# Zero products ahead of the first input, and two more PSUM banks for the first stage, in a spectral-filter and MLP kernel

## The chip, the cores and the metric

The kernel runs on one core of a Trainium2 chip. The metric is the device time of one execution in microseconds (us), the median of several executions. Times inside a profile count from the start of its span.

## The reference

```python
# x: (8, 3008, 256); filt_r, filt_i: (1505, 256); w_in: (256, 2048); w_out: (2048, 256); alpha: (2048)
X = np.fft.rfft(x, axis=1)
y = np.fft.irfft(X * (filt_r + 1j * filt_i), n=3008, axis=1).reshape(24064, 256)
h = y @ w_in
s = np.sin(alpha * h)
out = (h + s * s / (alpha + 1e-09)) @ w_out
```

The kernel does the Fourier transform as matrix products in three stages, batch by batch. Stage 1 (products `pa`) goes through a DRAM buffer (`d1`, stored from `t1`, reloaded as `t2`), stage 2 (products `pb` and `pc`, filter between them) goes through another (`d2`, reloaded as `t4`), and stage 3 (`pd`) gives `y`. Then come the hidden layer (`ph`, a sine, a square) and the projection (`po`). While the MLP of one batch runs, the three stages of the next are woven in between, following a plan in steps. Only the first batch's stages stand alone: they are the prologue.

## The kernel before

```python
fps = pool("fps", 2, PSUM); hps = pool("hps", 2, PSUM); ops = pool("ops", 2, PSUM)
...
def load_x(b):                       # four input chunks, cast to fp16 by the DMA, GpSimd queue
    for ch in range(4):
        ins = nc.gpsimd.dma_start(out=xt, in_=...)
        if b == 1:
            after(ins, marks["t4"])
...
def stage1(u):
    ch, half = divmod(u, 2)
    ...
    for i in range(2):
        n0 = 4 * half + 2 * i
        ps = fps.tile([128, 512], FP32, name=f"pa_{b}_{u}_{i}", tag="f")
        marks["pe"] = nc.tensor.matmul(out=ps[0:NK, :], lhsT=wf_t, rhs=st["x"][ch][:, n0:n0 + 2, :],
                                       start=True, stop=True)
        evac(st["t1"][:, n0:n0 + 2, :], ps[0:NK, :])      # ScalarE and VectorE in turn
    if half == 1:
        nc.sync.dma_start(out=d1_rows[:, 8 * ch:8 * ch + 8, :], in_=st["t1"])
    if u == 7:
        ...   # reload: t2[g], g = 0..3, one half each on the SyncE and (batch 0) the ScalarE queue
...
first = spectral(0)
for _, piece in first[:8]:           # stage 1 of batch 0
    piece()
after(nc.sync.dma_start(out=d_t, in_=d_dram.ap()), marks["x", 1])    # 768 KB table for stage 2
...
for g in range(4):                   # filter rows, GpSimd queue
    for k, filt in enumerate((filt_r, filt_i)):
        for q in range(2):
            ins = nc.gpsimd.dma_start(out=f_t[k][32 * q:32 * q + 32, 6 * g:6 * g + 6, :], in_=...)
            if g >= 2:
                after(ins, marks["t2", g - 2])
...
w_out32 = vpool.tile([128, 16, C], FP32, name="w_out32", tag="v")
after(nc.gpsimd.dma_start(out=w_out32, in_=...), marks["t4"])        # output weights, 2 MB
...
plan = {1: [-45 + i for i in range(8)],
        2: [-29 + 14 * i / 13 for i in range(13)],
        3: [-10, -9] + [-7 + 2 * i for i in range(14)]}
...
        at_step = 48 * b + plan[stage][at[stage]]
        if b == 1 and stage == 1:
            at_step = 9 + at[stage]
```

Of the kernel before, what the change touches and what calls it, by code (L numbers as in the profile page):

```python
# [9 lines left out]
FP16 = mybir.dt.float16  # L10
FP32 = mybir.dt.float32
# [43 lines left out]
def kernel(  # L55
# [10 lines left out]
    nc = tc.nc  # L66
# [17 lines left out]
    def pool(name, bufs, space=None):  # L84
        kw = {} if space is None else {"space": space}
        return ctx.enter_context(tc.tile_pool(name=name, bufs=bufs, **kw))

    cpool = pool("consts", 1)
# [10 lines left out]
    fps = pool("fps", 2, PSUM)  # L99
    hps = pool("hps", 2, PSUM)  # L100
    ops = pool("ops", 2, PSUM)
# [11 lines left out]
    def load_x(b):  # L113
        tiles = []
        for ch in range(4):
            xt = xpool.tile([NR, 8, C], FP16, name=f"x_{b}_{ch}", tag="x")
            ins = nc.gpsimd.dma_start(
                out=xt,
                in_=bass.AP(tensor=x.tensor, offset=x.offset + (b * S + ch * 8) * C,
                            ap=[[32 * C, NR], [C, 8], [1, C]]),  # L120
            )
            if b == 1:
                after(ins, marks["t4"])
            if b == 0:
                marks["x", ch] = ins
            tiles.append(xt)
        return tiles
# [3 lines left out]
    def evac(dst, src, on_act=None):  # L131
        flip[0] ^= 1
        if flip[0] if on_act is None else on_act:
            marks["act"] = nc.scalar.copy(out=dst, in_=src)
        else:
            marks["dve"] = nc.vector.tensor_copy(out=dst, in_=src)

    def spectral(b):
# [8 lines left out]
        def stage1(u):  # L147
            ch, half = divmod(u, 2)
            if u == 0:
                st["x"] = load_x(b)  # L150
            if half == 0:
                st["t1"] = t1pool.tile([NK, 8, C], FP16, name=f"t1_{b}_{ch}", tag="t1")
            for i in range(2):
                n0 = 4 * half + 2 * i
                ps = fps.tile([128, 512], FP32, name=f"pa_{b}_{u}_{i}", tag="f")
                marks["pe"] = nc.tensor.matmul(out=ps[0:NK, :], lhsT=wf_t, rhs=st["x"][ch][:, n0:n0 + 2, :],  # L156
                                               start=True, stop=True)
                evac(st["t1"][:, n0:n0 + 2, :], ps[0:NK, :])
# [3 lines that stand above are left out]
                st["t2"] = []  # L162
                for g in range(4):
                    t2 = t2pool.tile([128, 6, C], FP16, name=f"t2_{b}_{g}", tag="t2")
                    for p in range(2):
                        a0 = p * NS + 6 * g
                        eng = nc.scalar if b == 0 and p else nc.sync
                        marks["t2", g] = eng.dma_start(out=t2[64 * p:64 * p + 64, :, :],
                                          in_=d1[a0:a0 + 6, :, :].rearrange("s n c -> n s c"))
                    st["t2"].append(t2)  # L170
# [53 lines left out]
        for u in range(8):  # L224
            pieces.append((1, lambda u=u: stage1(u)))
# [11 lines left out]
    warm = cpool.tile([128, 1], FP32)  # L237
    nc.vector.memset(warm, 0.0)
    nc.scalar.activation(out=warm, in_=warm, func=AFT.Sin)

    first = spectral(0)
    for _, piece in first[:8]:
# [12 lines left out]
    for i in range(2):  # L255
        al_row.append(opool.tile([128, 2, C], FP32, name=f"al_row_{i}", tag="o"))
        for h in range(2):
            nc.scalar.dma_start(
                out=al_row[i][64 * h:64 * h + 1].rearrange("p a b -> p (a b)"),
# [10 lines left out]
    for g in range(4):  # L270
        for k, filt in enumerate((filt_r, filt_i)):
            for q in range(2):
                off, step = ((6 * g) * C, C) if q == 0 else ((N1 - 6 * g) * C, -C)
                ins = nc.gpsimd.dma_start(  # L274
                    out=f_t[k][32 * q:32 * q + 32, 6 * g:6 * g + 6, :],
# [20 lines left out]
    ps = fps.tile([128, 512], FP32, name="ps_rec", tag="f")  # L296
# [3 lines left out]
    for i in range(2):  # L300
        al_bc.append(hps.tile([128, 2, 512], FP32, name=f"al_bc_{i}", tag="h"))
        for h in range(2):
            behind(nc.tensor.matmul(out=al_bc[i][:, h, :], lhsT=ones[64 * h:64 * h + 1, :],
                                    rhs=al_row[i][64 * h:64 * h + 1].rearrange("p a b -> p (a b)"),
                                    start=True, stop=True), s1_pe)
# [17 lines left out]
    for i in range(2):  # L323
        for cb in range(2):
            behind(nc.vector.tensor_tensor(
                out=w1[:, cb, 1024 * i:1024 * i + 1024], in0=w_in32[:, cb, 1024 * i:1024 * i + 1024],
# [152 lines left out]
```

## Time and profile before

| | before |
|---|---|
| time, median of 3 (range) | 883.07 us (882.7 to 884.4) |
| span of the profiled run | 881.2 us |
| last store of stage 1: issued | 17.30 us |
| reload of it: issued | 22.49 us |
| first stage-2 product | 26.86 us |
| output weights first used | 64.38 us |
| first projection product | 74.19 us |
| first stage-2 product of batch 1, TensorE's wait before it | 104.19 us, 3.15 us |

The busy times by stretch follow. The columns after the length are busy us and number of instructions for TensorE, its weight loads, VectorE, ScalarE and GpSimd, then the granted TensorE clock, the DMA share (1.00 is all 16 engines busy) and GB/s.

```profile
core 0: us, PE busy (x) PEld busy (x) DVE busy (x) ACT busy (x) POOL busy (x), PEclk, DMA share, GB/s
...
11.00:16.00 5.00, 3.67 (x9) 1.27 (x8) 2.75 (x4) 2.13 (x4) 0.57 (x1) 1.00 1.05 274
16.00:22.00 6.00, 6.00 (x30) 3.55 (x31) 4.30 (x9) 2.91 (x4) 0.00 (x0) 1.00 1.05 286
22.00:24.00 2.00, 2.00 (x6) 0.66 (x2) 1.05 (x3) 0.25 (x1) 0.00 (x0) 1.00 0.01 4
...
200.00:800.00 600.00, 599.71 (x4553) 424.73 (x4551) 357.31 (x625) 375.97 (x482) 178.33 (x346) 1.00 0.42 102
```

From 200 to 800 us TensorE rests 0.29 us in all, so there is little to shorten but the prologue. In the prologue the DMA engines are full until 22 us and then empty for two: the reload may be issued only when the last store has landed (issued at 22.49 us), and its first bytes move 1.3 us later, near 23.8 us.

The chain of waits that ended last, in order of time (start, length, what):

```profile
14.57 0.60 PE pa_6_1_163 L156
15.16 0.02 issue
15.19 0.70 DVE t_0_3_159 L136
15.89 0.04 issue
15.93 0.60 PE pa_7_1_169 L156
16.53 0.02 issue
16.55 0.70 DVE t_0_3_159 L136
...
17.30 5.03 DMA d_0_107<-t_0_3_159
...
23.21 4.29 DMA t_0_1_176<-d_0_107
...
52.01 12.34 DMA w_out_502<-in_moe_w_out_dram
```

Product and eviction alternate one by one, which is what two banks allow when VectorE owns one of them. The store after them takes 5.03 us for 384 KB.

### The profile page before, as it was taken

How to read it: one execution, taken by the hardware profiler on the slowest of the kernel's cores; microseconds unless marked ns; L12 is line 12 of the kernel's file. 1: busy time of each engine (PE TensorE's matmuls, PEld its weight loads, DVE VectorE, ACT ScalarE, POOL GpSimd, SP SyncE). 2: the span in 40 equal slices, each digit the busy share in tenths (PEclk: the TensorE clock that was granted, in tenths of full speed). 3: DMA queues.
4: the chain of work that ended last, by engine and by line, in shares of the span. 5: the costliest groups of instructions: out<-in, count | busy, mean ns of one | idle time of the engine just before them, and what ended most of it. 6: DMA issues, size and time to landing. Idle time of an engine off the chain costs nothing.

```text
span 881.2 us, 15647 instructions
## 1 busy us (share of the span) xinstructions
PE 839.1 (95%) x6233; PEld 585.2 (66%) x6233; DVE 503.9 (57%) x886; ACT 521.1 (59%) x671; POOL 255.3 (29%) x495
## 2 busy tenths in 40 slices
PE   6759899999999999999999999999999999999993
PEld 2336677667776677767776677767776677667673
DVE  4737575566646565465756566565755666455441
ACT  4545565566656665666656666566656666555550
POOL 3211223333233232332233323233232232333332
PEclk9969999999999999999999999999999999999997
DMA  9984834185334724175343823256242533311111
GB/s 217 246 236 87 194 79 108 51 171 119 84 110 114 156 69 117 54 152 123 79 123 91 179 71 99 75 131 150 68 115 67 134 77 79 108 37 33 36 42 32
DMA packets 82737, 94.99 MB, mean 108 GB/s; under 512 B 12700, under 2 KB 64932, under 8 KB 82664
## 3 DMA queue, kind: packets, MB, share of 16 engines
q1 hardware_dynamic: 57008, 50.36, 22.0%
q0 software_dynamic: 23728, 42.77, 21.7%
q10 hardware_dynamic: 1928, 0.86, 0.5%
q8 instruction: 49, 0.80, 0.4%
q14 instruction: 24, 0.20, 0.1%
HBM read 58.02 MB, written 49.81 MB: 122 GB/s over the span
## 4 chain that ended last, share of the span: by engine, by line
PE 89%; DMA 6%; DVE 2%; issue 1%; ACT 0%; POOL 0%; SPq 0%; POOLq 0%; DVEq 0%
DMA w_out_502<-in_moe_w_out_dram 1%; DMA t_1_0_939<-d_1_504 1%; DMA d_7_517<-g_9_8756 1%; DMA d_0_107<-t_0_3_159 1%; DMA x_0_109<-in_x_dram 1%; DMA t_7_0_8931<-d_7_517 1%; DMA t_0_1_176<-d_0_107 0%; DMA t_0_0_476<-d_0_108 0%; PE po_0_5494 L390 0%; PE po_0_7950 L390 0%; PE po_2_4348 L390 0%; PE po_2_838 L390 0%; PE po_2_1892 L390 0%; PE po_0_705 L390 0%; PE po_0_4463 L390 0%
## 5 line engine op out<-in xcount | busy, mean ns | idle before, releaser
L375 PEld LDWEIGHTS <-w_465 128*128 128x128 f16 x1536 | 150.3, 98 | 100.4 <-issue 2.3
L198 PEld LDWEIGHTS <-e_t 128*128 128x128 f16 x384 | 37.5, 99 | 12.8 <-issue 2.5
L394 PEld LDWEIGHTS <-y 128*128 128x128 f16 x376 | 36.7, 98 | 4.7
L179 PEld LDWEIGHTS <-d_t 128*128 128x128 f16 x192 | 18.7, 100 | 27.6 <-DMA t_0_0_173<-d_0_107 3.5
L156 PEld LDWEIGHTS <-wf_t 94*96 94x96 f16 x128 | 16.5, 129 | 18.8 <-issue 9.4
L380 DVE TENSOR_TENSOR v_9644<-v_9644 128x1024 f16<-128x1024 f16 x8 | 5.5, 693 | 8.0 <-ACT v_9644 L379 8.0
L380 DVE TENSOR_TENSOR v_9789<-v_9789 128x1024 f16<-128x1024 f16 x8 | 5.5, 693 | 8.0 <-ACT v_9789 L379 8.0
L380 DVE TENSOR_TENSOR v_9488<-v_9488 128x1024 f16<-128x1024 f16 x8 | 5.5, 693 | 7.7 <-ACT v_9488 L379 7.7
L380 DVE TENSOR_TENSOR v_3898<-v_3898 128x1024 f16<-128x1024 f16 x8 | 5.5, 691 | 7.1 <-ACT v_3898 L379 7.1
L380 DVE TENSOR_TENSOR v_8810<-v_8810 128x1024 f16<-128x1024 f16 x8 | 5.5, 690 | 7.1 <-ACT v_8810 L379 7.1
L380 DVE TENSOR_TENSOR v_2681<-v_2681 128x1024 f16<-128x1024 f16 x8 | 5.5, 690 | 7.1 <-ACT v_2681 L379 7.1
L380 DVE TENSOR_TENSOR v_7593<-v_7593 128x1024 f16<-128x1024 f16 x8 | 5.5, 690 | 7.1 <-ACT v_7593 L379 7.1
L380 DVE TENSOR_TENSOR v_6354<-v_6354 128x1024 f16<-128x1024 f16 x8 | 5.5, 690 | 7.1 <-ACT v_6354 L379 7.1
L380 DVE TENSOR_TENSOR v_1442<-v_1442 128x1024 f16<-128x1024 f16 x8 | 5.5, 690 | 7.1 <-ACT v_1442 L379 7.1
L380 DVE TENSOR_TENSOR v_5137<-v_5137 128x1024 f16<-128x1024 f16 x8 | 5.5, 690 | 7.1 <-ACT v_5137 L379 7.1
L380 DVE TENSOR_TENSOR v_1608<-v_1608 128x1024 f16<-128x1024 f16 x8 | 5.5, 693 | 7.1 <-ACT v_1608 L379 7.1
L380 DVE TENSOR_TENSOR v_6520<-v_6520 128x1024 f16<-128x1024 f16 x8 | 5.5, 693 | 7.1 <-ACT v_6520 L379 7.1
L380 DVE TENSOR_TENSOR v_8976<-v_8976 128x1024 f16<-128x1024 f16 x8 | 5.5, 692 | 7.1 <-ACT v_8976 L379 7.1
L380 DVE TENSOR_TENSOR v_9147<-v_9147 128x1024 f16<-128x1024 f16 x8 | 5.5, 692 | 7.1 <-ACT v_9147 L379 7.1
L380 DVE TENSOR_TENSOR v_9317<-v_9317 128x1024 f16<-128x1024 f16 x8 | 5.5, 692 | 7.1 <-ACT v_9317 L379 7.1
L380 DVE TENSOR_TENSOR v_4064<-v_4064 128x1024 f16<-128x1024 f16 x8 | 5.5, 692 | 7.1 <-ACT v_4064 L379 7.1
L274 POOL DMA_DIRECT2D filt_101<-in_filt_r_dram x8 | 4.6, 587 | 16.9 <-DMA t_0_0_173<-d_0_107 15.0
(2527 smaller groups left out, 2688.4 us busy)
## 6 DMA issues: line engine op xcount, KB each, us to landing
w_in_469<-in_moe_w_in_dram POOLq DMA_DIRECT2D x2, 1024.0 KB, 9.2
w_out_502<-in_moe_w_out_dram POOLq DMA_DIRECT2D x1, 2048.0 KB, 12.3
filt_101<-in_filt_r_dram POOLq DMA_DIRECT2D x8, 96.0 KB, 7.0
filt_102<-in_filt_i_dram POOLq DMA_DIRECT2D x8, 96.0 KB, 7.4
d_t<-d_tbl SPq DMA_DIRECT2D x1, 768.0 KB, 7.9
d_0_107<-t_0_0_117 SPq DMA_DIRECT2D x1, 384.0 KB
d_0_107<-t_0_1_131 SPq DMA_DIRECT2D x1, 384.0 KB, 6.5
d_0_107<-t_0_2_145 SPq DMA_DIRECT2D x1, 384.0 KB
```

The source lines that it names most:

```text
L156: marks["pe"] = nc.tensor.matmul(out=ps[0:NK, :], lhsT=wf_t, rhs=st["x"][ch][:, n0:n0 + 2, :], start=True, stop=True)
L179: nc.tensor.matmul(out=ps[:, i, :], lhsT=d_t[:, s, :], rhs=st["t2"][s // 6][:, s % 6, :], start=True, stop=True)
L198: nc.tensor.matmul(out=ps[:, i, :], lhsT=e_t[:, k, 2 * w + i, :], rhs=pr[k][:, i, :], start=(k == 0), stop=(k == 1))
L274: ins = nc.gpsimd.dma_start(out=f_t[k][32 * q:32 * q + 32, 6 * g:6 * g + 6, :], in_=bass.AP(tensor=filt.tensor, offset=filt.offset + off, ...
L375: marks["hidden"] = nc.tensor.matmul(out=ps[:, i, 0:n], lhsT=w1[:, cb, jb * 128:jb * 128 + 128], rhs=y_cols[:, cb, c0:c0 + n], start=(cb = ...
L380: marks["square"] = nc.vector.tensor_tensor(out=vs, in0=vs, in1=vs, op=ALU.mult)
L394: nc.tensor.matmul(out=dst, lhsT=y_cols[:, cb, c0 + 128 * t:c0 + 128 * t + 128], rhs=m_t[:, cb, :], start=False, stop=(cb == 1))
```

## The change

Its intent: feed TensorE with products of zeros from 1.2 us on, so that its clock is up when the first input lands near 6 us; and let stage 1 of the first batch run on four banks, two for each evicting engine, so that product and eviction overlap.

```diff
-                ps = fps.tile([128, 512], FP32, name=f"pa_{b}_{u}_{i}", tag="f")
+                ps = (ops if b == 0 and i else fps).tile(
+                    [128, 512], FP32, name=f"pa_{b}_{u}_{i}", tag="o" if b == 0 and i else "f")
@@
+    zeros = cpool.tile([128, 512], FP16)
+    nc.vector.memset(zeros, 0.0)
+    idle = hps.tile([128, 2, 512], FP32, name="idle", tag="h")
+    for i in range(12):
+        nc.tensor.matmul(out=idle[:, 0, :], lhsT=zeros[:, 0:128], rhs=zeros, start=True, stop=True)
+
     first = spectral(0)
```

## The prediction

> **What bounds the kernel now.** Busy times by stretch: TensorE works 599.71 of the 600 us from 200 to 800, at clock 1.00. The change touches none of that, only the prologue (first 70 us), where the chain of waits runs through DMAs: first input load 1.25 to 5.92 us; stage 1 until 17.25, its last steps repeating product 0.60, VectorE eviction 0.69, on two PSUM banks; last store of stage 1 17.30 to 22.33; reload until 27.5; stage 2, bound by VectorE (4.9 of each 5 us); store, reload, 12.34 us load of the output weights; TensorE from 69 us.
>
> **What the change does.**
> - Twelve 128x512 products of zeros. Such products take 0.58 us in stage 1 and 0.38 later, so the clock is halved at first although the clock row prints 1.00. In stage 1 unhindered products start 0.38 to 0.43 apart, so twelve take about 5.1 us from about 1.3, ending near 6.4; if the clock rises meanwhile, near 5.6. The Trainium skill ("TensorE: Matmul & The Clock Gate", "What's actually happening") says about 3.4 us of sustained work lifts it; here full speed comes at 31.2 us, after 2.6 us of dense products. The input lands at 5.9: at worst stage 1 starts 0.5 us late, absorbed.
> - Four banks: two for ScalarE (0.58 us), two for VectorE (0.69). Four products (one input chunk) need about 1.4 us instead of 2.7. But chunks land 1.9 us apart (5.9, 7.7, 9.5, 11.4), so stage 1 becomes bound by input. Its last store is issued near 13.5 to 14.0 instead of 17.30.
>
> **How much is on the critical path.** Hardly any, because that store does not wait only for its issue. The DMA share is 1.0 or more from 4 to 21 us. The SyncE queue holds, in order, the 768 KB table (issued 7.74, landed 15.9) and the four 384 KB stores (issued 9.14, 11.85, 14.58, 17.30). It moves nothing until 11 us, while the input loads fill the engines, then 0.14 to 0.29 MB every microsecond until 21.8, 2.37 MB in all: exactly table and stores. The second store landed at 18.35, so the queue was never empty when the last came. The Trainium skill ("DMA: Bandwidth & Descriptors", "Queues, rings and completion order") says an engine consumes a ring in order and takes turns between queues by packet[...]. Earlier issues lengthen the backlog; the last landing moves only as far as stores get ahead of the filter loads on GpSimd's queue (0.25 MB between 19 and 21 us, at 0.3 MB per us at most 0.8 us: an estimate). I expect 0.5 us, and perhaps 0.3 from warmer products at 28 to 31 us, where VectorE is nearly full anyway. What is gained there passes down the chain.
>
> **Prediction.** 883.07 - 0.9 = 882.2 us; 8 in 10 between 879.8 and 883.6. Faster by over 2%: 0.005; within 2%: 0.99; slower: 0.005.
>
> **What would show it.** Stage 1's last eviction ends near 13.5 to 14 instead of 17.25 (banks). The last store, issued early, lands at 21.5 to 22.3, its wait grown from 5.0 to about 8 us (backlog). First stage-2 product at 26.3 to 26.9 (before: 26.86). TensorE from 100 us on unchanged.
>
> **What would make it wrong.** If the stores overtake filter loads or table, or deeper queues move more bytes per microsecond, the gain could reach 2 to 3.5 us. If earlier stores delay the table (needed at 16.3) or filter rows, or the zeros outlast the input, it could be 0.5 us slower.

## The result, and the profile after

The changed kernel took 881.20 us (880.19 to 882.96, 4 runs) against 883.74 us (882.7 to 885.41, 4 runs). The ratio is 0.9972, with a 95% interval of 0.9948 to 0.9995. A ratio is the mean time of one kernel's fast runs over the mean of the other's in the same rounds, so it is not quite the ratio of the medians. The same stretches after the change:

```profile
core 0: us, PE busy (x) PEld busy (x) DVE busy (x) ACT busy (x) POOL busy (x), PEclk, DMA share, GB/s
...
11.00:16.00 5.00, 4.18 (x9) 1.25 (x9) 3.38 (x5) 1.66 (x4) 0.57 (x1) 0.59 1.07 276
16.00:22.00 6.00, 6.00 (x31) 3.40 (x31) 2.94 (x7) 2.96 (x3) 0.00 (x0) 0.50 1.06 290
22.00:24.00 2.00, 0.87 (x3) 0.00 (x0) 0.87 (x3) 0.00 (x0) 0.00 (x0) 0.50 0.28 81
...
200.00:800.00 600.00, 600.00 (x4556) 425.38 (x4555) 357.27 (x625) 376.37 (x482) 177.33 (x344) 1.00 0.42 101
```

The DMA engines work at the same rate up to 22 us (276 and 290 GB/s against 274 and 286). The clock column cannot be compared here: in the profile of the kernel before the clock records begin at 31.2 us, and a stretch without a record is printed as 1.00, although its products take 0.58 us; with the zeros the records begin at 5.1 us. The chain:

```profile
2.95 8.96 DMA x_3_130<-in_x_dram
...
11.95 0.66 PE pa_6_0_175 L158
12.62 0.43 PE pa_7_0_181 L158
13.04 0.43 PE pa_6_1_178 L158
13.47 0.43 PE pa_7_1_184 L158
13.90 2.00 PE al_bc_274 L313 x2
...
20.80 0.97 ACT e_t L296
...
21.89 4.25 DMA t_0_0_188<-d_0_122
...
51.66 12.65 DMA w_out_517<-in_moe_w_out_dram
```

Stage 1 now waits for its last input, as forecast. The chain no longer names the store, but that is a coincidence: a ScalarE eviction of stage-2 tables happens to end at the time of the store's landing, 21.8 us. What released both halves of the reload is the landing. SyncE's half is issued at 21.87 and ScalarE's at 21.89 us, and in twelve of the fourteen profiles ScalarE's half follows SyncE's by 0.02 us, whenever that eviction ends (in zeros only it ends 0.1 us after the issue). The store and the first use of its data, VectorE's first use of the output weights, and TensorE's wait in batch 1, before and after:

```profile
17.30 0.30 SPq L160 DMA_DIRECT2D d_0_107<-t_0_3_159  x1
...
26.86 0.61 PE L179 MATMUL pb_0_267<-t_0_0_173,d_t 128*128 128x256 f16 x2 [1.97 <-DMA t_0_0_173<-d_0_107]
...
64.38 1.14 DVE L338 TENSOR_SCALAR w_466<-w_out_502,rec_t 128x256 f16<-128x256 f32 x4 [2.30 <-DMA w_out_502<-in_moe_w_out_dram]
...
104.19 0.38 PE L179 MATMUL pb_0_1020<-t_1_0_939,d_t 128*128 128x256 f16 x2 [3.15 <-DMA t_1_0_939<-d_1_504]
```

```profile
14.86 0.30 SPq L162 DMA_DIRECT2D d_0_122<-t_0_3_174  x1
...
26.19 0.61 PE L181 MATMUL pb_0_282<-t_0_0_188,d_t 128*128 128x256 f16 x2 [3.32 <-DMA t_0_0_188<-d_0_122]
...
64.33 1.14 DVE L348 TENSOR_SCALAR w_481<-w_out_517,rec_t 128x256 f16<-128x256 f32 x4 [2.85 <-DMA w_out_517<-in_moe_w_out_dram]
...
102.66 0.38 PE L181 MATMUL pb_0_1035<-t_1_0_954,d_t 128*128 128x256 f16 x2 [1.67 <-DMA t_1_0_954<-d_1_519]
```

The number in brackets is the idle time of the engine before the instruction. The last store is issued 2.44 us earlier, and stage 2 starts only 0.67 us earlier. At the output weights 0.05 us of that is left, and then 1.5 us appear at batch 1's reload, and 0.5 us near 754 us at that of a later batch, which the change does not touch. So this one pair of profiles puts most of its 2.0 us difference in a place that has nothing to do with the change, and the experiments had to tell whether that was its doing.

### The profile page after: what moved, and what is told of

It reads as the page before. It is cut to its first block, busy times and chain, and to the rows that moved or that the text cites. A ratio compares the mean times of both kernels' runs of the same rounds, so it can differ in the third digit from the quotient of the medians.

```text
span 879.2 us, 15673 instructions
## 1 busy us (share of the span) xinstructions
PE 840.8 (96%) x6245; PEld 586.7 (67%) x6245; DVE 503.8 (57%) x887; ACT 520.6 (59%) x671; POOL 255.1 (29%) x495
## 3 DMA queue, kind: packets, MB, share of 16 engines
q0 software_dynamic: 23728, 42.77, 21.8%
## 4 chain that ended last, share of the span: by engine, by line
PE 91%; DMA 5%; DVE 1%; ACT 1%; issue 1%; POOL 1%; SPq 0%; POOLq 0%; DVEq 0%; ACTq 0%
DMA w_out_517<-in_moe_w_out_dram 1%; DMA x_3_130<-in_x_dram 1%; DMA t_0_0_491<-d_0_123 0%; DMA t_1_0_954<-d_1_519 0%; DMA t_0_0_188<-d_0_122 0%; PE al_bc_274 L313 0%; PE po_0_7965 L400 0%; PE po_0_5509 L400 0%; PE po_2_6819 L400 0%; PE po_2_1907 L400 0%; PE po_0_720 L400 0%; PE po_2_4363 L400 0%; PE po_0_3053 L400 0%; PE po_0_2022 L400 0%; PE po_0_9170 L400 0%
```

## The experiments

Twelve kernels ran, all with correct results, in three groups of four; a group shared a chip and 11 runs of the kernel before. Theory A: the DMA backlog lets only 0.6 us or so through, the rest of the difference is scatter of later waits. Theory B: the change gains 2 us or more each time, by way of batch 1's reload. Each kernel has one profile. These are its waypoints in us; "before" and "changed" are the two kernels above:

| kernel | first `pa` | reload issued | first `pb` | weights used | first `po` | wait in batch 1 |
|---|---|---|---|---|---|---|
| before | 5.96 | 22.49 | 26.86 | 64.38 | 74.19 | 3.15 |
| before, again | 5.96 | 22.49 | 26.63 | 64.78 | 74.59 | 2.82 |
| before, shift | 6.11 | 22.47 | 26.78 | 64.77 | 74.58 | none |
| before, shift, input held | 6.10 | 22.54 | 26.95 | 64.40 | 77.43 | 0.48 |
| changed | 6.42 | 21.87 | 26.19 | 64.33 | 74.14 | 1.67 |
| changed, again | 6.32 | 21.39 | 25.50 | 62.81 | 72.62 | 3.14 |
| changed, shift | 6.18 | 21.73 | 26.10 | 64.56 | 74.36 | 0.40 |
| changed, shift, input held | 6.33 | 22.03 | 26.26 | 63.62 | 76.78 | 1.15 |
| zeros only | 6.45 | 22.64 | 27.30 | 63.84 | 73.65 | 1.94 |
| zeros only, shift | 6.43 | 22.65 | 27.02 | 65.38 | 75.18 | 1.01 |
| banks only | 6.12 | 22.33 | 26.47 | 64.42 | 74.23 | 2.31 |
| banks only in order, shift | 5.96 | 21.54 | 25.65 | 64.79 | 74.60 | 0.18 |
| before, shift, filter held | 6.09 | 20.52 | 28.21 | 65.73 | 75.54 | none |
| changed, shift, filter held | 6.30 | 20.73 | 25.75 | 64.16 | 73.97 | none |

### Changed kernel again

No edit.

> The changed kernel once more. Theory A (the prologue's gain is about 0.6 us at the first stage-2 product, and is lost again in the wait for the output weights; the 2 us that the two profiles differ by come from batch 1's reload, 4.37 us against 5.85, whose length varies from run to run): the first stage-2 product near 26.2 us, the first psm product within 0.4 us of the kernel before, the TensorE wait before pb_0 of batch 1 anywhere from 1.5 to 3.3 us, and a ratio between 0.996 and 1.001. Theory B (the gain of 2 to 2.5 us belongs to the change and is the same each time): TensorE wait before batch 1's pb_0 again 1.5 to 1.9 us and a ratio of 0.9965 to 0.998.

Measured: 882.35 us (881.13 to 882.81) against 883.80 us, ratio 0.9974 (0.9942 to 1.0005). The first stage-2 product came at 25.50 us, 0.7 earlier than theory A had it, and the first `po` 1.6 us before that of the first profile of before, so here the prologue's gain did pass the output weights. The wait in batch 1 was 3.14 us: theory B's repeat of 1.5 to 1.9 us did not come (nor does the interval, which reaches 1, show a gain by itself).

### Kernel before again

No edit.

> The kernel before, unchanged, as a control: ratio 1.000 within 0.002 under both theories. Theory A: its profile's TensorE wait before batch 1's first stage-2 product is not again 3.15 us but anywhere from 1.5 to 3.3. Theory B: again 2.9 to 3.3 us. Output weights used from 69 us under both.

Measured: 883.74 us (880.16 to 884.97) against 883.80 us, ratio 0.9985 (0.9954 to 1.0017). By the medians the two are alike; the ratio is below one because one of the 11 runs of the other took 891.08 us. The wait in batch 1 was 2.82 us, just outside theory B's range. With it, and in the changed kernel's repeat, came something new. The instruction that ended the wait in this profile, and the busy times of the stretches after it:

```profile
104.25 0.58 PE L179 MATMUL pb<-t,d_t 128*128 128x256 f16 x2 [2.82 <-DMA t<-d]
```

```profile
104.00:105.00 1.00, 0.75 (x7) 0.65 (x8) 0.00 (x0) 0.07 (x1) 0.56 (x2) 0.50 1.26 221
105.00:106.00 1.00, 1.00 (x7) 0.68 (x6) 0.81 (x2) 0.51 (x1) 0.00 (x0) 0.50 1.26 249
106.00:107.00 1.00, 1.00 (x6) 0.59 (x4) 1.00 (x3) 0.00 (x0) 0.00 (x0) 0.50 1.06 274
```

The two products take 0.58 us here and 0.38 us in the first profile of before: the clock (0.50) had fallen during the wait. It can be priced. From the first `po` to the start of the last two `po` products TensorE does the same work in every kernel, so that time, less the waits, should be nearly constant. It is 866.89 - 74.19 - 3.15 - 0.29 = 789.26 us in the first profile of before and 864.85 - 74.14 - 1.67 = 789.04 us in the changed kernel. It is 867.87 - 74.59 - 2.82 = 790.46 us here and 866.25 - 72.62 - 3.14 = 790.49 us in the changed kernel's repeat. These two are also the only ones of all fourteen profiles in which the clock fell there; in the ten not named here the same sum gives 789.05 to 789.77 us. A wait of 2.8 to 3.2 us in batch 1 was therefore followed by a further loss of 0.7 to 1.4 us in two of three cases, and by none in one.

### Zeros only

```diff
-                ps = (ops if b == 0 and i else fps).tile(
-                    [128, 512], FP32, name=f"pa_{b}_{u}_{i}", tag="o" if b == 0 and i else "f")
+                ps = fps.tile([128, 512], FP32, name=f"pa_{b}_{u}_{i}", tag="f")
```

> Only the twelve products of zeros, two banks as before. Both theories: the products of stage 1 take 0.38 us while the clock stays up, but two banks still make each pair wait for VectorE (about 1.1 us a pair instead of 1.36, if the clock stays up; 1.36 if it falls), so the last store is issued at 15 to 17 us and the SyncE queue drains at 21.3 to 21.8 as before. First stage-2 product at 26.3 to 26.9. Time: theory A 0 to 1 us under the kernel before, the same as with banks alone; theory B, if the zeros are what gains, 2 us under.

Measured: 883.14 us (880.83 to 884.71), ratio 0.9982 (0.9951 to 1.0012). First stage-2 product at 27.30 us, later than expected and than in any profile of the kernel before (26.63 to 26.95 us). The zeros ran until 6.3 us and the input landed near 6.4 us; the clock was at 0.71 between 9 and 10 us and at 0.50 from 10 us on. With two banks the pairs then take 1.36 us again.

### Banks only

```diff
-    zeros = cpool.tile([128, 512], FP16)
-    nc.vector.memset(zeros, 0.0)
-    idle = hps.tile([128, 2, 512], FP32, name="idle", tag="h")
-    for i in range(12):
-        nc.tensor.matmul(out=idle[:, 0, :], lhsT=zeros[:, 0:128], rhs=zeros, start=True, stop=True)
```

> Only the four banks, no products of zeros. Products take 0.58 to 0.63 us, start 0.43 apart, still under the 1.9 us between inputs for four: last store issued at 14.2 to 15 us, as with the whole change, first stage-2 product at 26.0 to 26.5. So the banks alone give the whole 0.6 us at that point. Time: theory A, 0 to 1 us under the kernel before plus the chance of batch 1's reload; theory B, 2 to 2.5 us under.

Measured: 883.50 us (881.11 to 885.19), ratio 0.9987 (0.9956 to 1.0018). The last store was issued at 16.6 us, not at 14.2 to 15, because this kernel is not the clean half it was meant to be. Without the zeros the scheduler put a broadcast of alpha ahead of stage 1's last product:

```profile
13.29 2.07 PE L307 MATMUL al_bc<-al_row,ones 1*128 1x512 f32 x2
...
15.29 0.66 PE L158 MATMUL pa<-x,wf_t 94*96 94x512 f16 x1
```

Even so, the reload was issued at 22.33 us, just 0.16 before the 22.49 of before: 0.7 us of earlier issue brought almost nothing. The clean version is run below.

### Batch 1's stage 2 two steps later, kernel before

This takes the wait in batch 1 away by giving TensorE other work meanwhile ("shift").

```diff
             if b == 1 and stage == 1:
                 at_step = 9 + at[stage]
+            if b == 1 and stage == 2:
+                at_step = 21 + at[stage]
```

> The kernel before with stage 2 of batch 1 planned two steps later (first piece at step 21, one a step, ending at 33 as before), so that TensorE has hidden-layer work to do while batch 1's reload is in flight. The wait of TensorE before batch 1's first stage-2 product, 3.15 and 2.8 us in the two profiles of the kernel before, falls under 0.5 us; the time falls by 2 to 3 us against the kernel before (ratio 0.9965 to 0.998). If the wait only moves to a later place (stage 3 of batch 1), the ratio stays above 0.999.

Measured: 882.10 us (881.07 to 882.68) against 883.67 us, ratio 0.9978 (0.9961 to 0.9995). By the medians that is 1.6 us less, where 2 to 3 us were expected. The wait is gone, 0.7 us of small waits came up later (half of it near 549 us, at a later batch's reload, in the line below), and the range of the runs is 1.6 us where the kernel before has 4.3 us (881.56 to 885.89) in the same rounds.

```profile
549.19 0.34 PE L218 MATMUL pd<-wi_t,t 96*128 96x94 f16 x4 [0.34 <-DMA t<-d]
```

### The same shift, changed kernel

The same edit to the changed kernel.

> The changed kernel with the same shift. Theory A (the change's gain is whatever reaches TensorE past the wait for the output weights, 0 to 1.5 us, and batch 1's reload only adds noise): wait before batch 1's first stage-2 product under 0.5 us, ratio to the kernel before 0.995 to 0.9975, that is 0 to 1.5 us under the kernel before with the same shift. Theory B (the change gains 2 to 2.5 us by shortening batch 1's reload): with that wait gone in both, no difference to the kernel before with the same shift (within 0.5 us).

Measured: 880.49 us (880.20 to 881.23), ratio 0.9962 (0.9946 to 0.9979). With the wait away in both, 1.6 us remain between the medians. Theory B, by which batch 1's reload makes the gain, falls. Theory A's range (0 to 1.5 us) was just exceeded, and its other half, that the rest is scatter, is not shown: with the wait gone the first `po` comes only 0.22 us earlier than in the partner.

### Input of batch 1 held back until the output weights have landed

On the kernel before, with the shift:

```diff
             if b == 1:
                 after(ins, marks["t4"])
+                after(ins, marks["w_out"])
@@
-    after(nc.gpsimd.dma_start(out=w_out32, in_=...), marks["t4"])
+    marks["w_out"] = nc.gpsimd.dma_start(out=w_out32, in_=...)
+    after(marks["w_out"], marks["t4"])
```

> The kernel before with that shift, and with the input loads of batch 1 held back until the output weights have landed, so that these do not share the DMA engines. The weights, issued at 52 us, are first used about 2 us earlier than 64.4 us (their own 2 MB at 0.34 MB per us are 6 us), the input of batch 1 lands near 70 to 71 us, before it is needed near 76. Time 1.5 to 2 us under the kernel before with the shift alone (ratio to the kernel before 0.994 to 0.997). If the weights are not what TensorE waits for from 61 to 69 us, no gain over the shift alone.

Measured: 884.60 us (883.01 to 885.35), ratio 1.0004 (0.9985 to 1.0022): 2.5 us worse than the shift alone. The forecast was wrong twice. The weights took 11.7 us instead of 12.3 us although nothing of the input shared the engines with them, and were first used at 64.40 us, not 2 us earlier. And the scheduler had batch 1's first product ahead of the products that need the weights:

```profile
69.42 0.42 PE L157 MATMUL pa<-x,wf_t 94*96 94x512 f16 x1 [3.03 <-DMA x<-in_x_dram]
...
71.05 2.63 PE L357 MATMUL psm<-w,w1T 128*128 128x256 f16 x12
```

The same edit to the changed kernel:

> The changed kernel with both. With both later waits shortened, what the change gains in the prologue should come through whole: first stage-2 product 0.6 to 1.1 us earlier than in the kernel before with both, weights first used 0.6 to 1.1 us earlier, time 0.6 to 1.1 us less. Ratio to the kernel before 0.993 to 0.996. If the prologue's gain is lost in the weights' load whatever shares the engines, the two differ by under 0.3 us at the first psm product.

Measured: 883.28 us (882.19 to 884.33), ratio 0.9991 (0.9972 to 1.0010). As versions both failed. As a pair they say again what the change does: first stage-2 product 0.69 us earlier, weights 0.78 earlier, first `po` 0.65 earlier, time 1.3 us less by the medians.

### Half of the early filter rows held back until the last store has landed

On the kernel before, with the shift. This takes about 0.36 MB off the GpSimd queue while stores and table are moving.

```diff
-                nc.sync.dma_start(out=d1_rows[:, 8 * ch:8 * ch + 8, :], in_=st["t1"])
+                marks["d1", b] = nc.sync.dma_start(out=d1_rows[:, 8 * ch:8 * ch + 8, :], in_=st["t1"])
@@
+                if g == 1:
+                    after(ins, marks["d1", 0])
                 if g >= 2:
```

> The kernel before with batch 1's stage 2 two steps later, and the filter rows of group 1 (four of the eight early filter loads, about 0.36 MB of the GpSimd queue's traffic between 11 and 22 us) held back until stage 1's last store has landed. Theory A (a backlog of the DMA engines, not the issue of the last store, sets when it lands): the store is still issued at 17.3 us but lands, and the reload is issued, 0.7 to 1.5 us earlier than 22.5 us, at 21.0 to 21.8. If instead a fixed latency after the issue counts (5 us), the reload is issued at 22.3 to 22.5 as before. What follows (stage 2 may then wait for the rows of group 1) is not forecast closely: ratio to the kernel before 0.994 to 1.001.

Measured: 883.34 us (881.91 to 884.41) against 883.13 us, ratio 1.0001 (0.9980 to 1.0022). The last store was issued at 17.4 us as before, and the reload at 20.52 us instead of 22.47 us, sooner than the range forecast. So 2 of the store's 5 us were queueing behind filter rows: with these out of its way it lands 2 us sooner. No time was gained, and the first stage-2 product came later, at 28.21 us instead of 26.78 us. The same edit to the changed kernel:

> The changed kernel with both. Last store issued at 13.6 to 15 us. Theory A: backlog shorter by the same filter rows, reload issued at 20.4 to 21.2 us instead of 21.4 to 22.0; the early issue now buys more than before (0.6 to 1.0 us against the kernel before with both). If stores had already overtaken all filter loads in the changed kernel, no gain against 21.4 to 22.0. Ratio to the kernel before 0.993 to 1.0.

Measured: 880.46 us (879.29 to 882.48), ratio 0.9971 (0.9950 to 0.9993). The last store was issued at 14.1 us, 3.4 us before that of its partner, and the reload at 20.73 us, 0.2 us after that of its partner. The forecast that the early issue would buy 0.6 to 1.0 us here was wrong, and instructively so. The reloads on the SyncE queue, first the kernel before with the shift alone, then the kernel before with both and the changed kernel with both:

```profile
22.47 2.67 SPq L168 DMA_DIRECT2D t<-d  x4
```

```profile
20.52 2.67 SPq L168 DMA_DIRECT2D t<-d  x4
```

```profile
20.73 2.68 SPq L170 DMA_DIRECT2D t<-d  x4
```

With the filter rows out of the way the SyncE queue has the engines nearly to itself from 18 us on (it takes 101% and 92% of them between 18 and 19 us) and has moved all but a few packets by 20 us in both. So its own bytes, table and four stores, are the limit in both, and the issue of the last store has no visible influence left. What the early issue buys in the changed kernel is a place ahead of filter rows. A second limit stands close behind: ScalarE's half of the reload goes out only after ScalarE has started its last eviction of stage-2 tables. In these two kernels it was issued 0.16 and 0.17 us after that start, later than SyncE's half. What follows in these two is less clear: the reload shares the engines with the rows held back, and the first stage-2 product comes at 28.21 us in one and at 25.75 us in the other. In the first, ScalarE's half of the reload was issued at 21.52 us and in the second at 21.13 us; that is not enough to explain 2.5 us, and it stays open.

### Banks only, products in order, with the shift

As banks only, and stage 1's products tied to their order:

```diff
+                prev = marks.get("pe")
                 marks["pe"] = nc.tensor.matmul(...)
+                if b == 0 and prev is not None:
+                    behind(marks["pe"], prev)
```

> Four banks without the zeros, batch 1's stage 2 two steps later, and stage 1's products held in their order (without the zeros alone the scheduler let a 2 us broadcast product go ahead of the last one). Last store issued at 14.2 to 15 us; first stage-2 product at 25.9 to 26.3 us, as in the changed kernel: the zeros have no part in it. Ratio 0.995 to 0.9975, the same as the changed kernel with the shift (0.9962) within 0.0015. If the zeros matter, first stage-2 product at 26.5 us or later, ratio as the kernel before with the shift (0.9978).

Measured: 880.44 us (878.81 to 882.04), ratio 0.9969 (0.9944 to 0.9993). Last store issued at 14.2 us, reload at 21.54 us, first stage-2 product at 25.65 us. Four banks alone reach what the whole change reaches at this point, and a little more than was forecast. But the first `po` comes at 74.60 us, no earlier than the 74.58 us of the kernel before with the shift: all of the 1.1 us was lost again on the way.

### Zeros only, with the shift

> Only the zeros, two banks, batch 1's stage 2 two steps later. Last store issued at 16.5 to 17.3 us, reload issued at 22.4 to 22.7, first stage-2 product at 26.6 to 27.3 us: no gain. Ratio 0.997 to 0.999, as the kernel before with the shift (0.9978).

The edit is that of zeros only and that of the shift. Measured: 880.42 us (878.20 to 881.40), ratio 0.9966 (0.9944 to 0.9988). Last store issued at 16.9 us, reload at 22.65 us, first stage-2 product at 27.02 us and first `po` at 75.18 us: no gain anywhere in the prologue, as expected. The time was nevertheless as low as that of the other two in the group, below the range expected. Its interval holds 0.9978, the ratio of the kernel before with the shift, so the times do not separate the two; the waypoints up to the first `po` do. A gain that zeros may bring later in the kernel is not excluded (see the total below).

## Why the prediction was right, and which sizes were off

The point forecast was 882.2 us; 881.20 us was measured, inside 879.8 to 883.6 and within 2%. That the time fell inside owes something to the width of the range: the mechanism forecast accounts for less than half of the measured difference, as the last points show.

**Stage 1 becomes bound by its input: right.** The last product waits for the last input, landed 11.9 us. The last eviction ended at 14.8 us instead of 13.5 to 14, because the input landed about 0.5 us later than before and the clock had fallen by then.

**The last store waits in a backlog: right.** Its issue moved by 2.44 us and its landing by 0.6 us; its wait grew from 5.0 to about 7 us. The 2 us that it lost with half of the filter rows gone, whatever its issue, show that queueing and not its issue set its landing. Four profiles of each kernel in the table (before, again, shift, input held) give the reload's issue as 22.50 us on average before and 21.76 us after: 0.74 us.

**The size of that, "I expect 0.5 us": mis-sized.** It measured 0.74 us, near the 0.8 us that the prediction gave as the most. The stores did get ahead of the filter rows. From 17 to 21 us the SyncE queue moved 0.17, 0.27, 0.14 and 0.15 MB in each microsecond before, and 0.24, 0.27, 0.29 and 0.18 after, the GpSimd queue's traffic slipping behind. Between 19 and 20 us, before and after (q1 is the SyncE queue, q0 GpSimd's; packets, MB, share of the 16 engines):

```profile
q0 software_dynamic: 156, 0.13, 78.9%
q1 hardware_dynamic: 51, 0.14, 39.2%
```

```profile
q1 hardware_dynamic: 87, 0.29, 77.7%
q0 software_dynamic: 84, 0.05, 31.5%
```

**"Perhaps 0.3 from warmer products at 28 to 31 us": wrong.** The zeros did lift the clock, and it did not stay up. Changed kernel, first its products in order of time, then its stretches, with the clock in the third column from the right:

```profile
1.23 4.64 PE L249 MATMUL idle<-zeros 128*128 128x512 f16 x12 [1.23 <-DVE zeros L246]
...
6.42 0.38 PE L158 MATMUL pa_0_0_133<-x_0_124,wf_t 94*96 94x512 f16 x1 [0.55 <-DMA x_0_124<-in_x_dram]
```

```profile
11.00:12.00 1.00, 0.19 (x2) 0.05 (x2) 1.00 (x2) 0.59 (x2) 0.00 (x0) 0.94 1.18 257
12.00:13.00 1.00, 1.00 (x3) 0.56 (x4) 0.25 (x1) 0.35 (x1) 0.57 (x1) 0.50 1.14 334
...
32.00:33.00 1.00, 1.00 (x9) 0.80 (x8) 0.53 (x2) 0.42 (x1) 1.00 (x2) 0.82 1.26 197
```

Products of 0.38 us instead of 0.59 start at 6.4 us; at 12 us the clock is back at a half. With four fast products every 1.9 us TensorE had been busy for only 3.2 of the 5.5 us before; that these gaps let the clock fall is inferred, no run tests it. It rises again at 32.4 us, and the products between 28 and 31 us take 0.42 us as before. (Over all profiles it rises at 30.8 to 33.8 us without the zeros and 30.5 to 33.5 us with them.) In the prologue the zeros bought nothing: banks alone in order started stage 2 at 25.65 us, zeros alone at 27.02 and 27.30 us. In the seven kernels with zeros the first product of stage 1 starts at 6.18 to 6.45 us, in the seven without at 5.96 to 6.12 us. The worry that the zeros might outlast the input explains this only in part: in the changed kernel's repeat they did (they end at 6.5 us, the input landed at 5.9), but in the changed kernel itself they end at 5.87 us and the input landed at 6.4. That is absorbed.

**"What is gained there passes down the chain": its direction fits, its size is not shown.** For the kernels before and changed, again, and with the shift, the first stage-2 product comes 0.83 us earlier on average (26.76 against 25.93) and the first `po` 0.75 us earlier (74.45 against 73.71). But one profile, that of the changed kernel's repeat, carries most of the second mean. Pair by pair it is 0.05, 1.97 and 0.22 us at the `po`, because the time between the two waypoints scatters from 46.35 to 48.95 us over all kernels without the held input, and with banks only in order nothing was left of 1.1 us.

**The total, 0.9 us: too small, but not by a known term.** Five pairs that differ by the change alone put it, by the medians, at 2.5, 1.4, 1.6, 1.3 and 2.9 us. The means at the first `po` put about 0.75 us of it in the prologue, an estimate from three profiles of each. Batch 1's wait and the fall of the clock that sometimes follows it add up to 4.5 us or as little as 1.7 us in a single run without the shift. They can lift or hide a difference of this size. Whether the change makes a long wait there rarer was not settled by two profiles of each kernel (3.15 and 2.82 us before, 1.67 and 3.14 us after). Nor was it settled why 1.3 us and more remain with the shift. The profiles show one place more. From the 561st `po` product, near 210 us, to the last, nine of the fourteen profiles take 653.71 to 653.75 us, all seven with the zeros among them. The other five, all without zeros, take 654.03 to 654.51 us, with waits of 0.15 to 0.57 us for a later batch's reload near 550 or 754 us. In the pair on record this is 0.5 of the 2.0 us. Whether the zeros do this or chance is not known.

**A faster version.** The shift gave the kernel before 1.6 us and the changed kernel 880.49 us, the tightest of all (1.0 us from lowest to highest), against 881.20 and 882.35 us for the changed kernel without it in other groups. Banks only in order with the shift measured the same (880.44 us) without the zeros. All are within 2% of both kernels.

## What to carry to other kernels

Before making a DMA start sooner, look at what its queue and the engines are doing at that time: with the engines full, an earlier issue buys only a place ahead of other traffic, here 0.74 us of 2.4 to 3.5 us. Deferring other traffic moved the landing further (2 us) than issuing sooner did, but in the kernel before gained no time. Before adding products of zeros, ask whether the work after them keeps TensorE busy enough to hold the clock; here 3.2 busy of 5.5 us did not. In a kernel of 883 us, read a gain of 1 us from waypoints in several profiles of each kernel; a single pair put the gain in the wrong place.

## What the Trainium skill lacked or had wrong

- "TensorE: Matmul & The Clock Gate", "HAM oscillation — how this bites in real kernels", gives as the rule that TensorE must have no idle gaps above about 3.4 us. In the changed kernel the clock fell to 0.50 at 12 us though no wait of TensorE since 6.4 us had been longer than 0.81 us; being busy for 3.88 of the 6 us before 11 was not enough. In waits of 2.82 and 3.14 us it fell too, and in one of 3.15 us it did not. The page does mention short idle spells, in its section on PSUM queues, without a number.
- The same page, "What's actually happening", has about 3.4 us of sustained work raise the clock. Before the change TensorE was busy for 4.65 and 4.90 us of the stretches 15 to 20 and 20 to 25 us, and its products still took 0.42 us instead of 0.27 until about 31 us. More than half of that work was fp32 products with one row of weights, and most of the rest transposes. The page says that transposes do not count as busy in the same way; of such fp32 products it says nothing.
- "DMA: Bandwidth & Descriptors", "Queues, rings and completion order", lets each engine take turns between queues. The table issued on the SyncE queue at 7.74 us moved nothing before 11 us, while the GpSimd queue's input loads took 101% to 109% of the engines: no share for 3.3 us, of which some 1.3 us are usual here between an issue and its first bytes (reload: 22.49 to 23.8 us). From 11 to 21 us both queues do move bytes in every microsecond. No page says that a queue can be held off so long.
- No page has anything on zeros ahead of the work and the first input's product, which started later in every profile with them: 5.96 to 6.12 us without, 6.18 to 6.45 us with. In part the zeros themselves ended later than the input landed, in part the input landed later, for a reason that was not found.
